# A speech codec's quantiser on one core: the reciprocal of Silu by another ScalarE function, PSUM given out bank by bank, and the order of the work from a table

## The chip, the cores and the metric

The kernel runs on one core of one Trainium2 chip. The core has five engines that run their own instruction queues in order: TensorE (PE in the profile, its weight loads PEld), VectorE (DVE), ScalarE (ACT), GpSimd (POOL) and SyncE (SP); sixteen DMA engines move data between HBM and SBUF. An engine that meets an instruction whose inputs are not there waits, and everything behind it in its queue waits too. The metric is the device time of the one core in microseconds, the median of several runs.

## What is computed

The input is two sequences of 16,000 tokens with 512 channels, in bf16. A depthwise convolution with three taps runs along the tokens, then Silu, then a residual quantiser with four codebooks of eight words, then a second depthwise convolution with three taps over the sum of the chosen words.

```python
z = sum(xp[:, i:i+T, :] * dw_enc[i] for i in range(3))
z = silu(z)
res, q = z, 0
for s in range(4):
    cb = codebooks[s]                      # 8 words of 512 channels
    d2 = |res|^2 - 2 res @ cb.T + |cb|^2
    sel = cb[d2.argmin(-1)]
    q, res = q + sel, res - sel
y = sum(qp[:, i:i+T, :] * dw_dec[i] for i in range(3))
```

## The kernel before

**Tiling.** Each of the 128 partition rows of the token matrix owns 250 consecutive tokens ("groups"). The groups are handled in 17 chunks of SIZES groups (12, thirteen times 16, 12, 12, 6). Within a chunk the 512 channels are four blocks of 128, and in the tiles the channels lie on the partitions.

**Front of a chunk (`load`, `front`).** SyncE issues transposing DMAs from HBM into XT. For each of the four blocks VectorE multiplies XT by the three taps (`product`, L673, into Z and T), and the sums Z + T are made by VectorE (L681) or by an accumulating DMA issued on GpSimd's queue (L679; the table DMA_ADDS says which). Then Silu: ScalarE takes E = Exp(-Z) (L685), VectorE adds one (`one`, L689), ScalarE takes LN = Ln(E) (L693) and E = Exp(-LN) (L696), which is the reciprocal, and VectorE multiplies RES = Z * E (`silu`, L701). The residual RES has three buffers, Z four, T five, E three, LN one. One table set with both Exp and Ln is loaded at the start (L309).

**Four stages of a chunk (`stage`).** In each, TensorE multiplies the residual by itself and by the code words (`score`, L761 and L769, up to six groups per PSUM tile of one bank); VectorE takes the largest entry per token as the norm (`norm`, L789, TR); the products with the words (`dots`, PR) are copied by ScalarE (L795) or by VectorE (L797), as DOTS says: for a chunk of 16 groups the first two pieces of six on ScalarE and the last of four on VectorE. VectorE then adds and takes the minimum (L822, L826, L832) and marks the chosen word (OH, L837). TensorE turns the marks (L848, in the last stage L854), VectorE copies them out of PSUM (`turned`, MT, L861), TensorE expands them (L870; last stage L865), ScalarE cuts them (PH, L879; OHT, L876). In the first three stages the residual is then changed in four blocks: in the blocks below ON_DVE TensorE makes the words (SEL, L906) and VectorE subtracts them (L916); in the others TensorE makes the new residual (NEW, L922 and L927) and ScalarE copies it back in two halves (`keep`, L934, L936). ON_DVE is 3 for all chunks but the last three, where it is 4.

**Output (`finish`, `outputs`).** TensorE multiplies the turned marks by tables of taps times words (Y, L971), ScalarE copies two groups at a time (YSB, L981), and SyncE stores (L984).

**PSUM.** Two pools: psG, two buffers of one bank for the scores, and psA, three buffers of two banks for everything else.

**What sets the order.** Every step is handed to `plan.add` with an engine, a holding time, the steps it needs, a due time and the buffers that it takes and gives. `Plan.run` passes a list scheduler forward and backward over them with the seeds in ROUNDS, shifts the ranks of some steps by the 531 seeds in MOVES, and `emit` then writes the steps out in that order; the engines' queues hold them as emitted. `emit` also fills gaps that the plan sees on TensorE with matmuls whose result is not used (`warm`, L548).

Of the kernel before, what the change touches and what calls it, by code (L numbers as in the profile page):

```python
# [12 lines left out]
F32 = mybir.dt.float32  # L13
# [16 lines left out]
DOTS = (1, 1, 0)  # L30

ON_DVE = [(3, 3, 3)] * 14 + [(4, 4, 4)] * 3
# [11 lines left out]
ZB, TB, EB, LNB, YB = 4, 5, 3, 1, 2  # L44
# [4 lines left out]
ROUNDS = [(11759, 1, 0, 0), (57303, 0.3, 1, 1), (5748, 1, 0.5, 1), (67857, 1, 1, 1), (38131, 0.3, 0, 1),  # L49
          (74597, 0.3, 0, 1)]  # L50

MOVES = [523166, 840848, 180453, 289372, 896190, 468587, 667483, 70738, 572357, 394540, 577496, 170691, 429993,
# [41 lines left out]

CELLS, COLUMNS, ROWS, QUARTERS = range(4)
WHOLE = (CELLS, CELLS, 0, 0.0)
SWITCH, CLING, SLOW = 0.1, 10.0, 1.08
RUNS, ADDS = (1, 1, 0, 0.0), (2, 2, 0, 0.0)
APART, CLUMP = 0.5, 2.0

LAG, SLACK, STORE = 2, 4.5, 0.35


class Plan:

    def __init__(self, slots):
        self.slots = dict(slots)
# [1000 lines left out]
```

## Time and profile before

| | us |
|---|---|
| median of 3 runs | 678.83 |
| lowest, highest | 675.73, 680.55 |
| span of the profiled execution, first to last instruction | 675.1 |
| DVE busy in it | 623.1 |
| ACT busy in it | 599.1 |
| PE busy in it | 541.9 |
| POOL busy in it | 105.4 |

Of the profiled execution only the span is recorded; the median of the runs lies 3.7 us above it, and the lowest run 0.6 us above it.

How to read the profile: a row of a group names the line of the kernel, the engine, the operation, the output and input tiles with their shapes, and the count; behind the first bar stand the microseconds in which the engine was busy with them and the mean of one in nanoseconds, behind the second the idle time of the engine just ahead of them and what ended it. Records on one engine overlap a little, so that the mean of one is larger than the distance from one start to the next.

### The profile page before, as it was taken

The numbers are of one execution on the slowest core, as the hardware profiler recorded it, in microseconds if no ns is written. First come the engines' busy times: TensorE is split into PE (matmuls) and PEld (weight loads), VectorE is DVE, ScalarE is ACT, GpSimd is POOL, SyncE is SP. The second block draws the span as 40 slices with busy tenths as digits, with TensorE's granted clock in tenths as the row PEclk, the third lists the DMA queues.
The fourth block names the chain that finished last, engine by engine and source line by source line (L and its number), as shares of the span: only waits on it lengthen the run. The fifth ranks groups of instructions, "written<-read, shape, count | busy, mean of one in ns | idle before, by whom it ended". The sixth has DMA issues, their size and how long they took to land.

```text
span 675.1 us, 25728 instructions
## 1 busy us (share of the span) xinstructions
PE 541.9 (80%) x11544; PEld 322.8 (48%) x11544; DVE 623.1 (92%) x1256; ACT 599.1 (89%) x615; POOL 105.4 (16%) x147
## 2 busy tenths in 40 slices
PE   6135866888988889797978898979898888989995
PEld 5023534545544535454544455545455455556551
DVE  6999999999999999899989999999999999999861
ACT  4869689999999999999988999999999899777566
POOL 8021112121111111020211102101112211110000
PEclk9668788999999999999999989999999999999998
DMA  6999898999999999999999897989979945353144
GB/s 155 153 199 193 146 195 145 159 230 178 189 235 158 224 201 180 188 241 213 188 198 185 202 187 186 198 185 165 228 140 182 238 78 137 97 126 125 69 182 194
DMA packets 164889, 119.38 MB, mean 177 GB/s; under 512 B 143801, under 2 KB 144186, under 8 KB 164650
## 3 DMA queue, kind: packets, MB, share of 16 engines
q1 hardware_dynamic: 150032, 69.88, 48.3%
q0 software_dynamic: 14464, 47.59, 38.9%
q8 instruction: 90, 1.47, 0.9%
q10 hardware_dynamic: 282, 0.26, 0.1%
q14 instruction: 21, 0.17, 0.1%
HBM read 2.36 MB, written 32.77 MB: 52 GB/s over the span
## 4 chain that ended last, share of the span: by engine, by line
DVE 47%; ACT 19%; DMA 13%; PE 13%; issue 7%; ACTq 0%; DVEq 0%; POOL 0%; POOLq 0%
DVE RES L916 13%; DMA Z<-T 8%; DVE RES L701 7%; DVE T L673 6%; DVE TR L789 6%; PE PS L769 4%; ACT YSB L981 4%; ACT E L696 4%; DVE Z L673 4%; ACT E L685 3%; DVE Z L681 3%; ACT LN L693 3%; DMA XT<-in_x_dram 3%; DVE E L689 3%; ACT RES L934 3%
## 5 line engine op out<-in xcount | busy, mean ns | idle before, releaser
L769 PE MATMUL PS<-RES 128*64 128x80 bf16 (+1 forms) x8064 | 180.3, 203 | 27.7 <-DVE RES L701 9.5
L769 PEld LDWEIGHTS <-RES 128*64 128x64 bf16 x8064 | 174.4, 115 | 38.2 <-DVE RES L916 10.6
L916 DVE TENSOR_TENSOR RES<-RES,SEL 128x2048 bf16<-128x2048 bf16 (+2 forms) x207 | 181.2, 907 | 5.3 <-PE SEL L906 4.8
L679 POOL DMA_DIRECT2D Z<-T x96 | 89.0, 976 | 492.6 <-DVE Z L673 64.2
L981 ACT ACTIVATE YSB<-Y 128x1024 bf16<-128x1024 f32 x126 | 127.1, 1054 | 13.7 <-PE Y L971 12.6
L685 ACT ACTIVATE E<-Z 128x2048 bf16<-128x2048 bf16 (+2 forms) x68 | 123.3, 1814 | 7.9 <-DMA Z<-T 4.2
L693 ACT ACTIVATE LN<-E 128x2048 f32<-128x2048 bf16 (+2 forms) x68 | 123.7, 1820 | 3.5 <-DVE E L689 3.1
L696 ACT ACTIVATE E<-LN 128x2048 bf16<-128x2048 f32 (+2 forms) x68 | 123.1, 1810 | 0.3
L789 DVE TENSOR_REDUCE TR<-PS 128x6 bf16<-128x384 f32 (+1 forms) x188 | 94.4, 506 | 16.3 <-PE PS L769 16.2
L673 DVE TENSOR_SCALAR T<-XT,WENC 128x2048 bf16<-128x2048 bf16 (+2 forms) x136 | 94.7, 706 | 5.8 <-DMA Z<-T 4.2
L934 ACT ACTIVATE RES<-NEW 128x1024 bf16<-128x1024 f32 x78 | 81.6, 1059 | 6.3 <-PE NEW L927 6.1
L701 DVE TENSOR_TENSOR RES<-Z,E 128x2048 bf16<-128x2048 bf16 (+2 forms) x68 | 77.2, 1136 | 0.8 <-ACT E L696 0.7
L906 PE MATMUL SEL<-PH,HIGH 64*128 64x512 bf16 (+2 forms) x324 | 61.6, 374 | 17.0 <-ACT YSB L981 5.9
L761 PE MATMUL PS<-MASK,IDENT 128*64 128x384 bf16 (+1 forms) x376 | 64.3, 337 | 11.8 <-ACT PR L795 6.6
L971 PE MATMUL Y<-S,OHT 64*128 64x512 bf16 (+1 forms) x186 | 55.3, 387 | 9.5 <-DVE RES L916 2.3
L906 PE MATMUL SEL<-PH,LOW 64*128 64x512 bf16 (+2 forms) x324 | 59.7, 360 | 0.0
L906 PE MATMUL SEL<-PH,MID 64*128 64x512 bf16 (+2 forms) x324 | 59.6, 360 | 0.0
L922 PE MATMUL NEW<-RES,IDENT 128*128 128x512 bf16 (+1 forms) x168 | 50.4, 382 | 9.8 <-DVE RES L916 3.4
L971 PE MATMUL Y<-T,OHT 64*128 64x512 bf16 (+1 forms) x187 | 53.7, 386 | 3.7 <-ACT OHT L876 1.8
L761 PEld LDWEIGHTS <-IDENT 128*64 128x64 bf16 x376 | 22.8, 109 | 58.8 <-issue 46.4
L673 DVE TENSOR_SCALAR Z<-XT,WENC 128x2048 bf16<-128x2048 bf16 (+2 forms) x68 | 47.7, 707 | 0.0
L689 DVE TENSOR_SCALAR E<-E 128x2048 bf16<-128x2048 bf16 (+2 forms) x68 | 44.3, 652 | 2.0 <-ACT E L685 1.9
(108 smaller groups left out, 584.2 us busy)
## 6 DMA issues: line engine op xcount, KB each, us to landing
Z<-T POOLq DMA_DIRECT2D x78, 512.0 KB, 6.3
out_dram<-YSB SPq DMA_DIRECT2D x61, 512.0 KB, 4.6
Z<-T POOLq DMA_DIRECT2D x12, 384.0 KB, 6.6
RES<-in_x_dram SPq DMA_DIRECT2D x1, 1664.0 KB, 7.2
Z<-T POOLq DMA_DIRECT2D x6, 256.0 KB, 5.3
XT<-in_x_dram SPq DMA_TRANSPOSE x76, 5.9
out_dram<-YSB SPq DMA_DIRECT2D x1, 384.0 KB, 2.3
out_dram<-YSB SPq DMA_DIRECT2D x1, 256.0 KB, 2.6
```

The lines of the kernel that those rows point to most:

```text
L673: nc.vector.tensor_scalar(out=places(u[name]), in0=taps(i, k), scalar1=WENC[:, i, k:k + 1], scalar2=None, op0=ALU.mult)
L685: nc.scalar.activation(u["E"][:, 0:G, :], u["Z"][:, 0:G, :], ACT.Exp, scale=-1.0)
L693: nc.scalar.activation(u["LN"][:, 0:G, :], u["E"][:, 0:G, :], ACT.Ln)
L696: nc.scalar.activation(u["E"][:, 0:G, :], u["LN"][:, 0:G, :], ACT.Exp, scale=-1.0)
L701: nc.vector.tensor_tensor(out=tokens(st["RES"], i, G), in0=halves(u["Z"]), in1=halves(u["E"]), op=ALU.mult)
L769: nc.tensor.matmul(V[d * HT:(d + 1) * HT, own - left:own + HT + right], lhsT=row[:, at:at + HT], rhs=row[:, at - left:at + HT + right], st ...
L789: nc.vector.tensor_reduce(out=to, in_=both(u["V", q], m, home, HT), axis=AX.X, op=ALU.max)
L906: nc.tensor.matmul(SEL[:, h, 0:W], lhsT=words[side(h), i * P:(i + 1) * P], rhs=u["PH"][side(h), :], start=(k == 0), stop=(k == len(parts) ...
L916: nc.vector.tensor_tensor(out=old, in0=old, in1=new, op=ALU.add)
L934: nc.scalar.activation(old, new.rearrange("p h (n t) -> p (h n) t", t=HT), ACT.Copy)
L971: nc.tensor.matmul(Y[:, h, :], lhsT=lhs()[rows], rhs=DEC[table][rows], start=(a == 0), stop=(a == len(banks[k][h][1]) - 1), skip_group_che ...
L981: nc.scalar.activation(u["YSB"][:, at:at + step * (n - 1) + 1:step, :], u[k][:, 0:n, :], ACT.Copy)
```

## The change

Four things change.

1. Silu's reciprocal: Ln and the second Exp go, and the LN pool with them; one ScalarE instruction with the function Reciprocal, with immediate bias and scale, stands in their place, in place on E. Exp and Reciprocal stand in different table sets, so that the build puts an ACT_TABLE_LOAD at each change from one to the other. The steps now need each other so that the four Exp of a chunk come ahead of its four Reciprocal, and these ahead of the next chunk's Exp: 34 loads in the program, where there was 1. Z has five buffers in place of four, E four in place of three.
2. PSUM is one tile of eight banks. A step says how many banks it holds (`banks`) and which step frees them (`frees`); the table PLACES gives the first bank of each step that takes any. The turned marks and their expansion share one bank, not two.
3. Work moves from VectorE to ScalarE: DOTS becomes (1, 1, 1), so that all pieces of PR are copied by ScalarE (68 more); the copy of the turned marks MT in the last stage goes to ScalarE (TURNED, 17); and in the second stage of five chunks ON_DVE becomes 2, so that five subtractions (L916) become ten copies on ScalarE (L934).
4. The scheduler, ROUNDS and MOVES are gone. A string, RANKS, gives each step a number; the steps are emitted in the order of the numbers. The matmuls of `warm` go into the bank of the step that takes banks next, and there are 41, where there were 65.

```diff
-DOTS = (1, 1, 0)
-ON_DVE = [(3, 3, 3)] * 14 + [(4, 4, 4)] * 3
+DOTS = (1, 1, 1)
+TURNED = (0, 0, 0, 1)
+ON_DVE = [(3, 3, 3), (3, 3, 3), (3, 3, 3), (3, 3, 3), (3, 2, 3), (3, 3, 3), (3, 2, 3), (3, 3, 3), (3, 2, 3), (3, 3, 3), (3, 2, 3), (3, 3, 3), (3, 2, 3), (3, 3, 3), (4, 4, 4), (4, 4, 4), (4, 4, 4)]
-ZB, TB, EB, LNB, YB = 4, 5, 3, 1, 2
+ZB, TB, EB, YB = 5, 5, 4, 2
...
+    def run(self):
+        digit = {c: n for n, c in enumerate(DIGITS)}
+        starts = [UNIT * (len(DIGITS) * digit[a] + digit[b]) for a, b in zip(RANKS[::2], RANKS[1::2])]
+        takers = [n for n, t in enumerate(self.tasks) if t[10]]
+        assert len(starts) == len(self.tasks) and len(takers) == len(PLACES)
+        self.emit(starts, sorted(range(len(starts)), key=lambda n: (starts[n], n)), dict(zip(takers, map(int, PLACES))))
...
-    psG = ctx.enter_context(tc.tile_pool(name="psG", bufs=2, space=bass.MemoryType.PSUM))
-    psA = ctx.enter_context(tc.tile_pool(name="psA", bufs=3, space=bass.MemoryType.PSUM))
-
-    nc.scalar.preload_act_table_set("natural_log_exp_and_others")
+    psum = ctx.enter_context(tc.tile_pool(name="psum", bufs=1, space=bass.MemoryType.PSUM))
+    PS = psum.tile([P, BANKS, 512], F32, name="PS")
+
+    nc.scalar.preload_act_table_set("exp_and_others")
...
-            def log():
-                u["LN"] = lnpool.tile([P, GC, P], F32, name="LN")
-                nc.scalar.activation(u["LN"][:, 0:G, :], u["E"][:, 0:G, :], ACT.Ln)
-
             def inverse():
-                nc.scalar.activation(u["E"][:, 0:G, :], u["LN"][:, 0:G, :], ACT.Exp, scale=-1.0)
+                e = u["E"][:, 0:G, :]
+                zero, unit = (mybir.ImmediateValue(dtype=F32, value=v) for v in (0.0, 1.0))
+                nc.scalar.add_instruction(mybir.InstActivation(
+                    func=ACT.Reciprocal, name=nc.get_next_instruction_name(), engine=mybir.EngineType.Activation,
+                    ins=[nc.scalar.lower_ap(e), zero, unit, zero], outs=[nc.scalar.lower_ap(e)]))
...
-            e = plan.add("ACT", act(1.8), act(1.8) + 0.12, [z], due, exp, take=("E",))
+            e = plan.add("ACT", act(1.8), act(1.8) + 0.12, [z] + kept.get("exps", [])[-1:] + kept.get("inverses", [])[-1:], due, exp,
+                         take=("E",), mode=EXPS)
+            kept.setdefault("exps", []).append(e)
             e = plan.add("DVE", dve(0.6), dve(0.6) + 0.1, [e], due, one)
-            e = plan.add("ACT", act(1.8), act(1.8) + 0.12, [e], due, log, take=("LN",))
-            e = plan.add("ACT", act(1.8), act(1.8) + 0.12, [e], due, inverse, give=("LN",))
...
+            def close():
+                r = plan.add("ACT", act(1.8), act(1.8) + 0.12, [e] + kept["exps"][-1:] + kept.get("inverses", [])[-1:], due, inverse, mode=INVERSES)
+                kept.setdefault("inverses", []).append(r)
...
-        for i in range(KT):
-            block(i)
+        for close in [block(i) for i in range(KT)]:
+            close()
...
-            nc.vector.tensor_copy(u["MT"], u["ps"][:, 0:n])
+            if TURNED[s]:
+                nc.scalar.activation(u["MT"], u["ps"][:, 0:n], ACT.Copy)
+            else:
+                nc.vector.tensor_copy(u["MT"], u["ps"][:, 0:n])
```

ScalarE's queue, from the second Exp of the sixth chunk on. E<-Z is the Exp, LN and E<-LN the Ln and the Exp of before, PR the products with the words, PH the cut marks, YSB the output and RES the copied-back residual. Before:

```order
L685 ACTIVATE E<-Z 128x2048
L934 ACTIVATE RES_94<-NEW 128x16x64
L795 ACTIVATE PR<-PS 128x8x6
L934 ACTIVATE RES_94<-NEW 128x16x64
L696 ACTIVATE E<-LN 128x2048
L879 ACTIVATE PH<-ps_oh 128x512
L693 ACTIVATE LN<-E 128x2048
L685 ACTIVATE E<-Z 128x2048
L795 ACTIVATE PR<-PS 128x8x6
L696 ACTIVATE E<-LN 128x2048
```

In the changed kernel the same place holds these rows; E<-E is the Reciprocal:

```order
L590 ACTIVATE E<-Z 128x2048
L706 ACTIVATE PR<-PS 128x8x6
L896 ACTIVATE YSB<-PS 128x1024
L590 ACTIVATE E<-Z 128x2048
L850 ACTIVATE RES_87<-PS 128x16x64
L706 ACTIVATE PR<-PS 128x8x6 x2
L590 ACTIVATE E<-Z 128x2048
L850 ACTIVATE RES_87<-PS 128x16x64
L706 ACTIVATE PR<-PS 128x8x4
L599 ACT_TABLE_LOAD
L599 ACTIVATE E<-E 128x2048
L706 ACTIVATE PR<-PS 128x8x4
```

Before, the reciprocal of one block stands among the Exp of the next blocks; now the first reciprocal of the chunk stands behind the fourth Exp and a table load, and the small copies PR of four groups stand in this queue.

VectorE's queue from the first product RES<-Z,E of the same chunk past the second. TR, V, KEY, M and OH are the steps from the norm to the marks, and RES<-RES,SEL or RES<-RES,PS the subtraction. Before:

```order
L701 TENSOR_TENSOR RES_94<-Z,E 128x2x16x64
L797 CAST PR<-PS 128x8x4
L673 TENSOR_SCALAR Z<-XT,WENC 128x2048
L822 TENSOR_TENSOR V<-PR,TR 128x128
L701 TENSOR_TENSOR RES_94<-Z,E 128x2x16x64
L916 TENSOR_TENSOR RES_93<-RES_93,SEL 128x2x16x64
L826 TENSOR_TENSOR KEY_132<-V,GWIDE 128x128
L789 TENSOR_REDUCE TR<-PS 128x4
L832 TENSOR_REDUCE M<-KEY_132 128x16
L797 CAST PR<-PS 128x8x4
L789 TENSOR_REDUCE TR<-PS 128x6
```

Now:

```order
L606 TENSOR_TENSOR RES_89<-Z,E 128x2x16x64
L700 TENSOR_REDUCE TR<-PS 128x6
L578 TENSOR_SCALAR Z<-XT,WENC 128x2048
L832 TENSOR_TENSOR RES_88<-RES_88,PS 128x2x16x64
L733 TENSOR_TENSOR V<-PR,TR 128x128
L606 TENSOR_TENSOR RES_89<-Z,E 128x2x16x64
L737 TENSOR_TENSOR KEY_123<-V,GWIDE 128x128
L578 TENSOR_SCALAR Z<-XT,WENC 128x2048
L743 TENSOR_REDUCE M<-KEY_123 128x16
L832 TENSOR_TENSOR RES_88<-RES_88,PS 128x2x16x64
L748 TENSOR_TENSOR OH_124<-KEY_123,M 128x128
L832 TENSOR_TENSOR RES_88<-RES_88,PS 128x2x16x64
```

The copies PR<-PS are gone from VectorE's queue, and V follows the last TR of its stage with work of other chunks between.

More of the change, by code (lines that the diff above doesn't have):

```diff
@@ L110, in __init__, with add @@
         self.part = 0
-    def add(self, engine, hold, delay, needs, due, emit, take=(), give=(), mode=WHOLE):
-        self.tasks.append((engine, hold, delay, [n for n in needs if n is not None], due, emit, take, give, mode, self.part))
+        self.bank = None
+    def add(self, engine, hold, delay, needs, due, emit, take=(), give=(), mode=WHOLE, banks=0, frees=None):
+        self.tasks.append((engine, hold, delay, [n for n in needs if n is not None], due, emit, take, give, mode, self.part, banks, frees))
@@ L245, in emit, with held @@
+    def emit(self, starts, order, place):
+        tasks = self.tasks
+        freed, spans, end = [0.0] * BANKS, [], 0.0
+        takers = [n for n in order if n in place]
+        def held(n):
+            return range(place[n], place[n] + tasks[n][10])
         for n in order:
-            engine, hold, delay, _, _, emit, take, give, _, _ = tasks[n]
+            engine, hold, delay, _, _, emit, _, _, _, _, banks, frees = tasks[n]
             at = starts[n]
@@ L259, in emit @@
                         end += 0.1
-                while back and back[0] <= at:
-                    free += 1
-                    heapq.heappop(back)
                 end = at + hold
                 spans.append((at, end))
-            free -= take.count("psG")
-            for _ in range(give.count("psG")):
-                heapq.heappush(back, at + max(hold, delay))
+            if banks:
+                takers.remove(n)
+                self.bank = place[n]
+                for b in held(n):
+                    freed[b] = 1e9
             emit()
+            if frees is not None:
+                for b in held(n if frees < 0 else frees):
+                    freed[b] = at + max(hold, delay)
 @with_exitstack
@@ L342 @@
     free = {"RES": list(RESB), "KEY": [], "OH": []}
[L343 removed]
+    plan = Plan({"XT": 2, "Z": ZB, "T": TB, "E": EB, "Y": YB, "RES": 3, "KEY": 3,
                  "OH": 3, "PH": PHB})
```

301 lines of the change are left out of this document (116 added, 185 removed), and 40 rows, old and new, of the table MOVES.

## The prediction

> **What bounds the kernel now.** I read the page's busy times and chain first, then a table of busy time by stretch, then what VectorE waits for. The first two lines are the page's; in the table of stretches the columns are the stretch, its length, the busy time of PE, PEld, DVE, ACT and POOL with instruction counts, the granted clock, the DMA engines' busy share and GB/s; the last block is who waited for whom on DVE from 40 to 600 us (total, times, longest).
>
> ```profile
> PE 541.9 (80%) x11544; PEld 322.8 (48%) x11544; DVE 623.1 (92%) x1256; ACT 599.1 (89%) x615; POOL 105.4 (16%) x147
> DVE 47%; ACT 19%; DMA 13%; PE 13%; issue 7%; ACTq 0%; DVEq 0%; POOL 0%; POOLq 0%
> ```
> ```profile
> 0.00:40.00 40.00, 12.74 (x117) 10.18 (x117) 33.18 (x81) 27.92 (x25) 15.56 (x48) 0.77 0.95 165
> 40.00:600.00 560.00, 466.32 (x10118) 275.83 (x10120) 538.47 (x1023) 519.43 (x522) 89.06 (x100) 0.97 0.95 184
> 120.00:520.00 400.00, 342.43 (x7574) 199.31 (x7570) 386.98 (x714) 386.83 (x391) 59.32 (x64) 1.00 1.01 193
> 600.00:675.10 75.10, 62.88 (x1321) 36.77 (x1315) 51.45 (x154) 51.71 (x70) 0.81 (x1) 0.97 0.35 132
> ```
> ```profile
> DVE TR L789 <- PE PS L769: 8.0, 11, 2.3
> DVE T L673 <- DMA Z<-T: 4.2, 3, 2.1
> DVE RES L916 <- PE SEL L906: 3.0, 8, 0.9
> DVE E L689 <- ACT E L685: 1.9, 3, 1.2
> DVE T L673 <- DMA XT<-in_x_dram: 1.5, 1, 1.5
> DVE RES L701 <- ACT E L696: 0.7, 1, 0.7
> DVE V L822 <- ACT PR L795: 0.7, 2, 0.4
> ```
>
> In the settled part, 120 to 520 us, VectorE and ScalarE are both busy for 387 of 400 us: two engines bound the kernel together, and the chain of waits changes between them. VectorE's idle time is 6.8 us before 40 us, 560 - 538.47 = 21.5 us in the middle and 75.1 - 51.45 = 23.7 us at the end, 52.0 us in all, which with 623.1 busy gives the span of 675.1. In the middle no single wait is large: 20.0 of the 21.5 us are the seven rows above, of which ScalarE releases 3.3. The DMA engines' share of 1.01 there says that the transfers are a third resource with little room. TensorE has room: 466 of 560 us.
>
> So a cut on ScalarE alone gives at most the few microseconds in which VectorE waits for it. What sets the gain is what VectorE itself loses.
>
> **VectorE.** The durations; the first rows are groups (busy, mean ns, then the idle time ahead), the others the timeline (start, length), from which the distance between starts is read, since records overlap.
>
> ```profile
> L797 DVE CAST PR<-PS 128x32 bf16<-128x32 f32 x56 | 10.1, 180 | 0.0
> L797 DVE CAST PR<-PS 128x48 bf16<-128x48 f32 x12 | 2.3, 195 | 0.0
> L861 DVE COPY MT<-ps_oh 128x512 bf16<-128x512 bf16 x13 | 5.4, 414 | 0.0
> L916 DVE TENSOR_TENSOR RES<-RES,SEL 128x2048 bf16<-128x2048 bf16 x117 | 140.1, 1212 | 3.4 <-PE SEL L906 3.1
> ```
> ```profile
> 323.23 0.18 DVE L797 CAST PR<-PS 128x32 bf16<-128x32 f32 x1
> 323.33 0.74 DVE L673 TENSOR_SCALAR Z<-XT,WENC 128x2048 bf16<-128x2048 bf16 x1
> ...
> 356.50 1.21 DVE L916 TENSOR_TENSOR RES<-RES,SEL 128x2048 bf16<-128x2048 bf16 x1
> 357.63 0.22 DVE L826 TENSOR_TENSOR KEY<-V,GWIDE 128x128 bf16<-128x128 bf16 x1
> ...
> 365.59 0.41 DVE L861 COPY MT<-ps_oh 128x512 bf16<-128x512 bf16 x1
> 365.92 0.41 DVE L789 TENSOR_REDUCE TR<-PS 128x4 bf16<-128x256 f32 x1
> ```
>
> A PR copy holds VectorE for 323.33 - 323.23 = 0.10 us, though its record is 0.18 long: 56 + 12 = 68 of them give 6.8 us. A copy MT of the last stage holds it for 0.33: 17, four of them smaller, give 5.5. A subtraction holds it for 1.13: five give 5.7. Together 18.0 us; every other VectorE step keeps its count and shape. Its busy time goes from 623.1 to 605.1.
>
> **ScalarE.** The removed Ln, the Exp, the one table load, and the timeline rows for what comes over from VectorE:
>
> ```profile
> L685 ACT ACTIVATE E<-Z 128x2048 bf16<-128x2048 bf16 x52 | 101.2, 1946 | 3.7 <-DMA Z<-T 2.0 <-DVE Z L681 1.6
> L693 ACT ACTIVATE LN<-E 128x2048 f32<-128x2048 bf16 x52 | 101.6, 1954 | 2.9 <-DVE E L689 2.7
> L693 ACT ACTIVATE LN<-E 128x1536 f32<-128x1536 bf16 x12 | 17.9, 1495 | 0.6 <-DVE E L689 0.5
> L693 ACT ACTIVATE LN<-E 128x1024 f32<-128x1024 bf16 x4 | 4.2, 1052 | 0.1
> L309 ACT ACT_TABLE_LOAD x1 | 1.3, 1283 | 0.7 <-PEq L1092 0.7
> ```
> ```profile
> 334.46 0.28 ACT L795 ACTIVATE PR<-PS 128x48 bf16<-128x48 f32 x1
> 334.56 1.99 ACT L693 ACTIVATE LN<-E 128x2048 f32<-128x2048 bf16 x1
> 336.36 0.29 ACT L795 ACTIVATE PR<-PS 128x48 bf16<-128x48 f32 x1
> 336.46 0.68 ACT L879 ACTIVATE PH<-ps_oh 128x512 bf16<-128x512 f32 x1
> 336.93 1.11 ACT L981 ACTIVATE YSB<-Y 128x1024 bf16<-128x1024 f32 x1
> ...
> 339.73 1.13 ACT L934 ACTIVATE RES<-NEW 128x1024 bf16<-128x1024 f32 x1
> 340.63 2.03 ACT L696 ACTIVATE E<-LN 128x2048 bf16<-128x2048 f32 x1
> ```
>
> A full Ln holds ScalarE for 1.80 us, 0.15 less than its mean record; by the same cut the smaller ones hold it for 1.35 and 0.90. So 52 x 1.80 + 12 x 1.35 + 4 x 0.90 = 113.4 us go. The Reciprocal is not in this trace. Ln and Exp, two functions with different output types, take 1954 and 1946 ns for the same tile, so I take it at the price of the second Exp whose place it has, no gain and no loss; the dear end is twice that, as if it ran in two passes, +113.4 us. Thirty-three more table loads cost 33 x 1.283 = 42.3 us if the record is the whole price. The trace has one load, with nothing ahead of it, so what a load costs between two busy instructions it doesn't show; as the dear end I take twice the record, 84.7 us, and below the record nothing, because it was busy that long. I take the record, the only row there is. Added: 68 PR at 0.10 = 6.8 us, 17 MT at no more than a PH's 0.47 = 8.0, ten residual copies at 0.90 = 9.0. The sum is -113.4 + 42.3 + 23.8 = -47.3: from 599.1 to 551.8 us busy, or to 594 at the dear load.
>
> The Trainium skill speaks against the record here: "ScalarE: Activation LUTs", section "What ACT_TABLE_LOAD costs", says that the 1283 ns of a load come with about 1380 ns in which the engine is drained, 2.66 us for each switch. By it 33 loads would cost an estimated 88 us, and ScalarE would stay at about 597. No run here shows the drain so far; the record of 1283 agrees with the first of the two figures.
>
> **Waits.** PR of a stage's last piece now comes from ScalarE. There a PR stands behind whatever is ahead of it in the queue, and on VectorE the step V and all behind it stand behind the PR. Of this wait there were 0.7 us in 2 times with 120 PR on ScalarE; with 188 I take about 1 us, and if ScalarE were late by one Exp (1.80) in each of the 68 stages it could be 122. The new bank plan lets the turned marks hold one bank and not two; what it can win is in the rows where VectorE waits for PS and SEL, 11.0 us together. TensorE gets ten NEW for five SEL and loses 24 unused matmuls; with 94 us of room in the middle I cost that at nothing. No step is added to the DMA queues.
>
> **The sum.** I leave VectorE's idle time at both ends, 6.8 + 23.7 us, since the last chunks keep ON_DVE at 4 and their chain of stages is the same length, and set the middle at 15 us in place of 21.5: the 3.3 that ScalarE released, as it gets 47 us of room, and some 3 of the 11.0 on PE. 605.1 + 6.8 + 23.7 + 15 = 650.6 us of span. The median lies 3.7 us above the span before (678.8 against 675.1), so the time is 654 us.
>
> **The rivals.** The rows for them: the landing time of the adding DMAs (lowest, median, highest), ScalarE's wait for them, and GB/s in 40 slices.
>
> ```profile
> DMA to landing us min/median/max: 3.3/6.2/12.6
> ```
> ```profile
> ACT E L685 <- DMA Z<-T: 4.2, 4, 2.2
> ```
> ```profile
> GB/s 155 153 199 193 146 195 145 159 230 178 189 235 158 224 201 180 188 241 213 188 198 185 202 187 186 198 185 165 228 140 182 238 78 137 97 126 125 69 182 194
> ```
>
> *A better order.* If the new order and the emptier ScalarE take the middle's idle time to 5 us and a third of the 30.5 at the ends, the span is 605.1 + 5 + 20 = 630 to 635: about 637. For it: the waits are small and scattered. Against: 23.7 us of them are at the end, where the last chunk's stages follow each other.
>
> *Dear table loads.* At 2.57 us a load ScalarE stays as full as before (594), nothing in VectorE's middle improves, and some waits grow: 605.1 + 52.0 = 657 to 664 of span, about 663. This is where the Trainium skill's drain would lead too.
>
> *The transfers bind.* The same bytes must move in less time. If the DMA share of 1.01 is the limit, the middle can't shrink, and the time stays near 677. Against it: slices up to 241 GB/s beside a mean of 193, and only 5.7 us of VectorE's waiting is on DMAs.
>
> *Slower: the fourth Exp holds up ScalarE.* All four Exp of a chunk must be issued before its first Reciprocal. The Exp of blocks 2 and 3 wait for two adding DMAs, which land in 6.2 us in the median and 12.6 at worst. When one is late, everything behind it in ScalarE's queue stands: PR, PH and the copied residual that VectorE and TensorE need, and all four Reciprocal, so that four products and with them the Z buffers are late. Before, a late Z held up one block. At 3 us in each of 14 chunks it costs 42 us: 696. It makes the kernel slower from (685.6 - 654) / 14 = 2.3 us a chunk on. For it: the DMA share, and the Z buffers that stay taken through both phases. Against: before, ScalarE waited 4.2 us in all for these DMAs, and there is a fifth Z and a fourth E.
>
> *The exchange doesn't save the Ln.* A Reciprocal at twice an Exp makes ScalarE 551.8 + 113.4 = 665 us busy; with the 12.1 and 23.4 us that it is idle at the ends the time is about 704. Only the missing row speaks for it. The Trainium skill, "ScalarE: Activation LUTs", section "Step-by-step: what each stage is for", has one element a cycle for every function, which by an estimate is the same price as an Exp; the equal rows of Ln and Exp agree.
>
> **The numbers.** A measurement of this kernel can tell 1% from no change: faster is below 672.0, slower above 685.6. Chances: the forecast 0.46 (its own range 645 to 665), the better order 0.17, dear loads 0.10, the transfers 0.11, the held-up queue 0.14, the dear Reciprocal 0.02. Faster are the first three, 0.72 with a hundredth off for the forecast's edge; the transfers' case and that hundredth give 0.12 within 1%; the last two 0.16. The range runs from the lowest end of the better order, 630 + 3.7 = 634, to 678, which takes in the first three cases (0.73) and most of the fourth.
>
> **What would show it.** Right: VectorE busy near 605 and over 97% between 120 and 500 us; ScalarE busy near 552 with 34 loads of 1.28 us and about 0.1 us of idle time around each; Reciprocal records of 1.95 us. Wrong: idle time around the loads of more than 1 us, which is the dear load; ScalarE's Exp waiting for Z<-T over 30 us in all, which is the held-up queue; VectorE's taps waiting for XT or Z<-T with GB/s no higher than 193, which are the transfers; V waiting for PR.

## The result and the profile after

The changed kernel is slower. The median is 682.49 us over 20 runs against 675.39 us over 20 runs of the kernel before on the same chip: a ratio of 1.0143, 95% interval 1.0110 to 1.0177, so 9.7 us more at 675. Ratios are of fast executions alone, those at most 1.5% above the fastest of their kernel (12 of 20 before, 19 of 20 now), and so this one is not the quotient of the two medians, which is 1.0105, or 7.1 us. Slower it is by both. The profiled execution has a span of 679.5 us against 675.1, and so shows 4.4 us of the loss.

The busy times (first line) and the chain that ended last (second line) of the changed kernel:

```profile
PE 537.8 (79%) x11513; PEld 324.4 (48%) x11550; DVE 605.9 (89%) x1166; ACT 555.2 (82%) x675; POOL 102.1 (15%) x147
DVE 40%; ACT 18%; PE 16%; DMA 15%; issue 9%; POOL 1%; SPq 0%; ACTq 0%; DVEq 0%; POOLq 0%
```

Its busy time by stretch, with the columns of the prediction's table:

```profile
0.00:40.00 40.00, 10.80 (x107) 9.91 (x108) 32.23 (x81) 18.62 (x14) 15.58 (x48) 0.69 1.02 165
40.00:600.00 560.00, 457.57 (x9918) 271.96 (x9946) 517.75 (x924) 478.77 (x569) 85.39 (x98) 0.95 0.95 180
120.00:520.00 400.00, 329.23 (x7150) 194.06 (x7176) 362.23 (x629) 349.65 (x414) 53.68 (x60) 0.96 1.00 188
600.00:679.50 79.50, 69.39 (x1490) 42.51 (x1496) 55.91 (x163) 57.85 (x93) 1.16 (x1) 0.96 0.40 151
```

VectorE's busy time is 605.9 us, as the sum had it (605.1), and ScalarE's 555.2 (551.8). What changed is idle time. VectorE's was 6.8, 21.5 and 23.7 us in the three parts of the span; it is now 40 - 32.23 = 7.8, 560 - 517.75 = 42.2 and 79.5 - 55.91 = 23.6. So 17.2 us of work went and 21.6 us of waiting came, nearly all of it (20.7) in the middle: together the 4.4 us between the two spans. Between 120 and 520 us neither engine is full any more: 362 and 350 of 400 us, where both were at 387.

What VectorE waits for in the middle of the changed kernel:

```profile
DVE TR L700 <- PE PS L680: 11.0, 11, 2.1
DVE T L578 <- DMA XT<-in_x_dram: 10.7, 2, 8.6
DVE RES L832 <- PE PS L822: 7.4, 9, 1.6
DVE Z L578 <- DMA XT<-in_x_dram: 5.3, 2, 4.1
DVE V L733 <- ACT PR L706: 1.8, 1, 1.8
DVE RES L606 <- ACT E L599: 1.3, 4, 0.7
DVE Z L586 <- DMA Z<-T: 0.8, 1, 0.8
```

The rows on XT have grown: 10.7 + 5.3 = 16.0 us against 1.5. The longest of them in the timeline of VectorE, with the idle time in brackets, and below it the pieces of the chain of waits that lead there:

```profile
429.42 0.22 DVE L775 COPY MT<-PS 128x128 bf16<-128x128 bf16 x1
438.20 0.75 DVE L578 TENSOR_SCALAR T<-XT,WENC 128x2048 bf16<-128x2048 bf16 x1 [8.56 <-DMA XT<-in_x_dram]
```
```profile
416.71 5.62 DMA Z<-T
422.33 0.02 issue
422.35 15.66 DMA XT<-in_x_dram
```

The transposing load could be issued only when an adding DMA had landed, because the two kinds take turns (`keep_apart`, LAG of 2), and it then took 15.66 us. That is far longer than the median landing of an XT load, 6.4 us. By an estimate from these rows a load of median length would have landed at 422.35 + 6.4 = 428.8, before VectorE was through with its copy at 429.42 + 0.22 = 429.64. So here the slow landing makes the wait, and the turn alone would not have. From 422.35 to 438.01 the DMA engines' busy share was 1.18, and they moved 123 GB/s where the mean from 120 to 520 us is 188. From issue to landing, the longest XT load took 11.1 us before and takes 15.1 here. SyncE's queue shows the waits for the turn over the whole span, a little longer than before; the first row is the changed kernel, the second the kernel before (total, times, longest):

```profile
SPq L507 <- DMA Z<-T: 219.1, 24, 17.9
```
```profile
SPq L602 <- DMA Z<-T: 196.2, 28, 14.8
```

ScalarE's new instructions, by group and then in the timeline around one switch from Exp (E<-Z) to Reciprocal (E<-E):

```profile
L599 ACT ACTIVATE E<-E 128x2048 bf16<-128x2048 bf16 x52 | 99.7, 1924 | 1.0 <-DVE E L594 0.9
L590 ACT ACTIVATE E<-Z 128x2048 bf16<-128x2048 bf16 x52 | 99.5, 1918 | 4.5 <-DVE Z L586 3.0 <-DMA Z<-T 1.3
L599 ACT ACT_TABLE_LOAD x17 | 21.8, 1283 | 0.3
L590 ACT ACT_TABLE_LOAD x16 | 20.5, 1283 | 3.4 <-DVE Z L586 3.0 <-DVE KEY L737 0.2
```
```profile
360.19 0.28 ACT L706 ACTIVATE PR<-PS 128x48 bf16<-128x48 f32 x1
360.49 1.28 ACT L599 ACT_TABLE_LOAD   x1
361.79 1.91 ACT L599 ACTIVATE E<-E 128x2048 bf16<-128x2048 bf16 x1
```

Reciprocal costs what Exp costs, 1924 against 1918 ns, and a load its record: the next instruction starts 361.79 - 360.49 = 1.30 us after it.

### The profile page after: what moved, and what is told of

Its sections match the earlier page's. It is cut to its first block, busy times and chain, and to the rows that moved or that the text cites. A ratio compares the mean times of both kernels' runs of the same rounds, so it can differ in the third digit from the quotient of the medians.

```text
span 679.5 us, 25822 instructions
## 1 busy us (share of the span) xinstructions
PE 537.8 (79%) x11513; PEld 324.4 (48%) x11550; DVE 605.9 (89%) x1166; ACT 555.2 (82%) x675; POOL 102.1 (15%) x147
## 2 busy tenths in 40 slices
DMA packets 164889, 119.38 MB, mean 176 GB/s; under 512 B 143801, under 2 KB 144186, under 8 KB 164650
## 4 chain that ended last, share of the span: by engine, by line
DVE 40%; ACT 18%; PE 16%; DMA 15%; issue 9%; POOL 1%; SPq 0%; ACTq 0%; DVEq 0%; POOLq 0%
DVE RES L832 11%; DMA XT<-in_x_dram 8%; DVE T L578 6%; PE PS L680 6%; DVE TR L700 6%; DMA Z<-T 5%; DVE RES L606 5%; ACT E L599 5%; PE PS L822 4%; ACT E L590 4%; ACT YSB L896 4%; DVE E L594 3%; DVE Z L578 3%; ACT RES L850 2%; DVE Z L586 2%
## 5 line engine op out<-in xcount | busy, mean ns | idle before, releaser
L832 DVE TENSOR_TENSOR RES<-RES,PS 128x2048 bf16<-128x2048 bf16 (+2 forms) x202 | 175.6, 902 | 10.3 <-PE PS L822 9.8
L896 ACT ACTIVATE YSB<-PS 128x1024 bf16<-128x1024 f32 x126 | 124.0, 1031 | 13.6 <-PE PS L886 8.6
L599 ACT ACTIVATE E<-E 128x2048 bf16<-128x2048 bf16 (+2 forms) x68 | 121.7, 1799 | 1.1 <-DVE E L594 0.9
L578 DVE TENSOR_SCALAR T<-XT,WENC 128x2048 bf16<-128x2048 bf16 (+2 forms) x136 | 94.9, 710 | 11.9 <-DMA XT<-in_x_dram 10.7
L850 ACT ACTIVATE RES<-PS 128x1024 bf16<-128x1024 f32 x88 | 89.9, 1032 | 7.4 <-PE PS L843 6.9
L822 PE MATMUL PS<-PH,HIGH 64*128 64x512 bf16 (+2 forms) x314 | 62.2, 381 | 12.2 <-ACT PH L793 4.2
L838 PE MATMUL PS<-RES,IDENT 128*128 128x512 bf16 (+1 forms) x188 | 58.1, 391 | 4.7 <-DVE RES L832 2.0
L822 PE MATMUL PS<-PH,LOW 64*128 64x512 bf16 (+2 forms) x314 | 59.7, 366 | 0.4 <-issue 0.4
L822 PE MATMUL PS<-PH,MID 64*128 64x512 bf16 (+2 forms) x314 | 59.7, 366 | 0.1
L886 PE MATMUL PS<-S,OHT 64*128 64x512 bf16 (+1 forms) x169 | 53.4, 397 | 6.1 <-DVE RES L832 2.7
L886 PE MATMUL PS<-T,OHT 64*128 64x512 bf16 (+1 forms) x170 | 51.9, 395 | 5.5 <-ACT OHT L790 1.8
```

The lines of the kernel that those rows point to most:

```text
L578: nc.vector.tensor_scalar(out=places(u[name]), in0=taps(i, k), scalar1=WENC[:, i, k:k + 1], scalar2=None, op0=ALU.mult)
L599: nc.scalar.add_instruction(mybir.InstActivation(func=ACT.Reciprocal, name=nc.get_next_instruction_name(), engine=mybir.EngineType.Activation,
L822: nc.tensor.matmul(SEL[:, h, 0:W], lhsT=words[side(h), i * P:(i + 1) * P], rhs=u["PH"][side(h), :], start=(k == 0), stop=(k == len(parts) ...
L832: nc.vector.tensor_tensor(out=old, in0=old, in1=new, op=ALU.add)
L850: nc.scalar.activation(old, new.rearrange("p h (n t) -> p (h n) t", t=HT), ACT.Copy)
L886: nc.tensor.matmul(Y[:, h, :], lhsT=lhs()[rows], rhs=DEC[table][rows], start=(a == 0), stop=(a == len(banks[k][h][1]) - 1), skip_group_che ...
```

## The experiments

Eighteen kernels ran, the kernel before beside each. "Ratio" is always to the kernel before; a difference between two runs is the difference of their ratios at 675 us, with the two intervals put together as the root of the sum of squares. The changed kernel stands at 1.0143.

### What of the work matters: loads, VectorE, transfers

**The table loads.** Exp in place of Reciprocal, so that no table is switched; the reciprocal is not computed.

```diff
-                    func=ACT.Reciprocal, name=nc.get_next_instruction_name(), engine=mybir.EngineType.Activation,
+                    func=ACT.Exp, name=nc.get_next_instruction_name(), engine=mybir.EngineType.Activation,
```

> The changed kernel with the function Exp where Reciprocal stood, so that the 33 table switches are gone (42 us of ScalarE) and the order is the same; Silu's reciprocal is not computed. Theory 'switches': 640-665, ratio 0.95-0.985. Theories 'transfers' and 'order': ScalarE's extra room is not used, 676-683, ratio 1.00-1.015.

Ratio 1.0124 (1.0050 to 1.0199): 1.3 us less than the changed kernel, plus or minus 5.6, with ScalarE at 516.3 us in place of 555.2. VectorE's waits for XT stay at 15.4 us. The switches as such are not what costs.

**VectorE and ScalarE lighter, in both kernels.** The subtractions and the copies of the residual work on half of the tokens (the other half keeps the residual of the stage before).

```diff
+                old = old[:, :, :, 0:HT // 2]
...
-                nc.scalar.activation(old, new.rearrange("p h (n t) -> p (h n) t", t=HT), ACT.Copy)
+                nc.scalar.activation(old[:, :, 0:HT // 2], new.rearrange("p h (n t) -> p (h n) t", t=HT)[:, :, 0:HT // 2], ACT.Copy)
```

> The changed kernel with the subtraction on VectorE and the residual copy on ScalarE over the first half of the tokens only, in the same order and with all DMAs: about 75 us less on VectorE and 38 less on ScalarE; the other half of the residual isn't changed. Theory 'transfers': the middle is held by the DMAs and hardly shrinks, 660-680, ratio 0.98-1.01. Theory 'order' or an engine as the bound: VectorE's cut shows for the most part, 610-645, ratio 0.90-0.955.

> The kernel before with the same halves left out. Theory 'transfers': it falls to the same floor as the changed kernel, 650-672, ratio 0.965-0.995, so that 75 us less on VectorE bring less than 25. Without a floor by the DMAs: 610-640, ratio 0.90-0.95.

The changed kernel: ratio 0.9950 (0.9910 to 0.9990). The kernel before: 0.9635 (0.9556 to 0.9714). Their busy lines, the changed kernel's first:

```profile
PE 538.7 (80%) x11513; PEld 320.9 (48%) x11550; DVE 540.2 (81%) x1166; ACT 520.9 (78%) x675; POOL 102.2 (15%) x147
```
```profile
PE 529.6 (82%) x11495; PEld 322.6 (50%) x11544; DVE 554.0 (86%) x1256; ACT 565.9 (88%) x615; POOL 106.6 (17%) x147
```

Both land where the theory of the transfers had them, the second just below its range. Two things follow. In the kernel before, 623.1 - 554.0 = 69.1 us less on VectorE (and 33 less on ScalarE) bring 24.6 us (plus or minus 5.3): VectorE alone does not bound it, and a microsecond taken from it is worth about 0.36, in an order of steps that was made for the full work (a new order for the light kernel was not tried). In the changed kernel 65.7 us less bring 13.0 (plus or minus 3.6), 0.20 for one, and with less work on both engines than the light kernel before it is 21 us slower. Both move the same bytes: the kernel before does so in a span of 645.1 us, so the transfers' capacity is no floor at 670. Something in the changed kernel holds it there that is neither an engine's work nor the sum of the bytes.

**The adding DMAs halved, in both kernels.** Only the first half of each tile is added.

```diff
-                    keep_apart(nc.gpsimd.dma_start(out=z, in_=t, accum_op=ALU.add), adds, runs)
+                    keep_apart(nc.gpsimd.dma_start(out=z[:, 0:G // 2, :], in_=t[:, 0:G // 2, :], accum_op=ALU.add), adds, runs)
```

> The changed kernel with the adding DMAs over the first half of each tile only: the same number of DMAs, half of their bytes (about 24 of 119 MB less); the other half of these sums is left out. Theory 'transfers': VectorE's 17 us come out and more, 645-665, ratio 0.955-0.985. Theory 'order': 674-682, ratio 1.00-1.012. 'Switches': as 'order'.

> The kernel before, with the adding DMAs over the first half of each tile only, the control to the same edit of the changed kernel. Theory 'transfers': before was bound by VectorE and ScalarE, so little goes: 665-673, ratio 0.985-0.998, and the changed kernel with the same edit is faster than this one. Theory 'order': about the same fall as in the changed kernel, which stays 5-10 us above this one.

Ratios 0.9672 (0.9589 to 0.9754) and 0.9878 (0.9796 to 0.9960): 31.8 us from the changed kernel, 8.2 from the kernel before, as the theory of the transfers had it. The changed kernel's middle with half the adding DMAs:

```profile
40.00:600.00 560.00, 477.27 (x10630) 285.24 (x10632) 542.50 (x994) 500.37 (x609) 89.62 (x99) 0.98 0.72 144
```

VectorE now idles 17.5 us there and not 42.2, and the changed kernel is 13.9 us (plus or minus 7.9) under the kernel before with the same halving. That is near the 17.2 us of work that VectorE lost: a gain is there as soon as the adding DMAs leave room.

**Which adding DMAs.** Blocks 0 and 1 of a chunk have one each, blocks 2 and 3 two. Halved for block 3 alone, or for blocks 0 and 1 alone: in both a third of the adding bytes loses its half. The first run's edit; the second has `i < 2`:

```diff
-                    keep_apart(nc.gpsimd.dma_start(out=z, in_=t, accum_op=ALU.add), adds, runs)
+                    m = G // 2 if i == 3 else G
+                    keep_apart(nc.gpsimd.dma_start(out=z[:, 0:m, :], in_=t[:, 0:m, :], accum_op=ALU.add), adds, runs)
```

> The changed kernel; the two adding transfers of the fourth token block of every chunk add the first half of the tile only (the other half of the transposed positions is not added). A third of the adding bytes goes. 'Z loop' (the next chunk's Z products wait for this chunk's Silu, whose four reciprocals wait for the fourth Exp, and that for two adding transfers one after the other): the loop gets shorter by two half transfers a chunk, so 12 to 25 us of the 29 us that halving all of them saved: 655 to 668 us. 'Bytes' (the transfers' capacity): a third of the 29 us, about 670 us, the same as the next run. 'VectorE binds': under 3 us.

> The changed kernel; the single adding transfers of the first two token blocks of every chunk (in the kernel's program these two blocks have fewer adding transfers than the last two) add the first half of the tile only. The same number of bytes goes as in the run before if each has one. 'Z loop': these Z are early and the fourth Exp does not wait for them: 0 to 5 us, 674 to 681 us. 'Bytes': as in the run before, about 670 us.

Ratios 0.9912 (0.9864 to 0.9960) and 0.9900 (0.9824 to 0.9976), 15.6 and 16.4 us less than the changed kernel. The theory of the Z loop had the second at 0 to 5 us and is wrong there: it makes no difference whose DMAs are shorter. That the two are alike is what the theory of the bytes had; by it each would be a third of the 31.8 us that halving all of them brought, 10.6, and both are somewhat more. VectorE's waits in the middle with blocks 0 and 1 halved:

```profile
DVE TR L701 <- PE PS L681: 12.5, 10, 2.7
DVE RES L833 <- PE PS L823: 7.7, 9, 1.6
DVE V L734 <- ACT PR L707: 2.4, 2, 1.9
DVE E L595 <- ACT E L591: 2.1, 4, 1.3
DVE T L578 <- issue: 1.1, 1, 1.1
DVE RES L607 <- ACT E L600: 1.0, 2, 0.7
DVE T L578 <- DMA Z<-T: 0.4, 1, 0.4
```

The waits for XT (16.0 us) are gone in both runs, those for TensorE are about as they were (18.4 us, here 20.2), and the time falls by the same 16 us. The longest landing of an XT load is 11.1 and 10.1 us, as in the kernel before or less. So the late XT loads are a place where this kernel loses, and it did not matter which third of the adding bytes was halved. The kernel before was not run with these two edits; with all adding DMAs halved it gained 8.2 us, so some of the 16 us it might gain too.

**The turns.** A transpose waits until the fourth-last adding DMA has landed, in place of the second-last, and the other way round.

```diff
-LAG, SLACK, STORE = 2, 4.5, 0.35
+LAG, SLACK, STORE = 4, 4.5, 0.35
```

> The changed kernel, with the take-turns rule between transposing and adding DMAs loosened: each waits for the fourth one back of the other kind, not the second (LAG 4 for 2). Theory 'transfers' (XT comes late because transposes stand behind adds that stand behind VectorE): VectorE's wait for XT falls from 16 us to under 5 and the time from 682 to 665-673, ratio to before 0.985-0.997. Theory 'order' (the fixed order loses the time in hand-overs between TensorE, ScalarE and VectorE): 679-685, ratio 1.007-1.018. Theory 'switches' (table loads and the four-and-four order on ScalarE): the same, 679-685.

Ratio 1.0764 (1.0662 to 1.0866), 41.9 us slower than the changed kernel; no theory had that. VectorE's waits for XT are gone, as the theory of the transfers had it, and SyncE waits less for its turn (95.0 us in place of 219.1), but the transfers get slower. Their issues, with count, size and the median time to landing, first in this run, then in the changed kernel:

```profile
Z<-T POOLq DMA_DIRECT2D x78, 512.0 KB, 7.6
...
XT<-in_x_dram SPq DMA_TRANSPOSE x76, 9.7
```
```profile
Z<-T POOLq DMA_DIRECT2D x78, 512.0 KB, 6.7
...
XT<-in_x_dram SPq DMA_TRANSPOSE x76, 6.4
```

ScalarE's Exp now waits 35.6 us for Z<-T (first row), where it was 1.5 in the changed kernel (second row), and VectorE's taps wait 20.9 us for it in the middle (third row, of this run):

```profile
ACT E L590 <- DMA Z<-T: 35.6, 8, 8.5
```
```profile
ACT E L590 <- DMA Z<-T: 1.5, 2, 1.3
```
```profile
DVE T L578 <- DMA Z<-T: 20.9, 7, 8.2
```

The turns cost waiting, but less than they save.

**Work back to VectorE.** PR of the last piece and MT back on VectorE; in another run one adding DMA in six back on VectorE.

```diff
-DOTS = (1, 1, 1)
-TURNED = (0, 0, 0, 1)
+DOTS = (1, 1, 0)
+TURNED = (0, 0, 0, 0)
```
```diff
-DMA_ADDS = [((), ())] + [((0, 1, 2, 3), (2, 3))] * 16
+DMA_ADDS = [((), ())] + [((0, 1, 2, 3), (3,))] * 16
```

> The changed kernel with one part undone in the same order of steps: PR of the last piece and MT of the last stage are copied by VectorE again (12 us more on VectorE, 15 less on ScalarE). Theory 'transfers': VectorE's time isn't what is short, 680-686, ratio 1.005-1.02, unchanged within 4 us. Theory 'VectorE binds' (the one of the prediction): 690-697, ratio 1.022-1.034.

> The changed kernel with the last sum Z + T of the third block taken from the DMAs and given to VectorE in 16 chunks (DMA_ADDS (3,) for (2, 3)): 16 adding DMAs less, about 17 us more on VectorE. Theory 'transfers': with a third of what halving all adds took off the DMAs, 669-677, ratio 0.992-1.004, below the changed kernel. Theory 'VectorE binds': 692-700, ratio 1.026-1.038.

Ratios 1.0270 (1.0164 to 1.0376) and 1.0251 (1.0165 to 1.0337). The first gives VectorE 12.3 us more and is 8.6 us slower (plus or minus 7.5): what was moved to ScalarE did not do the harm. The value lies in the range of 'VectorE binds' and over that of the transfers, though its uncertainty reaches both: work given back to VectorE costs 0.70 us for one, though work taken from it gained only 0.20. The second takes the XT waits away but gives VectorE 15.7 us more, and is 7.3 us slower (plus or minus 6.2): VectorE has too little room to take the additions over. That too is near 'VectorE binds' and over the range of the transfers, so neither theory holds for all of these runs: the late loads cost, and VectorE's work still counts.

### Batches, Z buffers and order under the old plan

To part the batches of four from the table and the single PSUM banks, the kernel before got parts 1 and 3 of the change only, with its own scheduler and pools and a new search of ROUNDS and MOVES.

**Batched, and not.** The second kernel has Exp in place of Reciprocal (not computed), so that no load and no batch is needed. Its Exp need no longer follow one another, and the first Silu product of a chunk is kept behind that of the chunk before.

```diff
-        for close in [block(i) for i in range(KT)]:
-            close()
+        for i in range(KT):
+            block(i)()
```

> The kernel before with its own planner, its PSUM pools and a new search of its order, and with two parts of the change: ScalarE's Reciprocal with four Exp and then four Reciprocal in a chunk, one more buffer for Z and for E, and the shifted copies (dot products, turned indices, subtraction). 'Z loop': the batching costs under this planner too: 670 to 690 us although VectorE has 18 us and ScalarE 47 us less to do than in the kernel before. 'Order and banks' (the new table and the single PSUM banks make the changed kernel slow): with the old plan the saving shows, 645 to 662 us.

> As the run before, with the same planner and an own search of the same length, but Exp stands in for Reciprocal (so no table changes and no batches: each block's second pass follows its own first; the reciprocal is not computed). Against the run before this takes away the batches and 42 us of table loads on ScalarE. 'Z loop': 640 to 660 us and at least 15 us under the run before. 'Order and banks': within 8 us of the run before (the loads alone had saved nothing in the changed kernel).

Ratios 1.0446 (1.0374 to 1.0519) and 0.9867 (0.9781 to 0.9953): 39.1 us apart, plus or minus 7.6, each some way above the range of the theory of the Z loop. So the batched Silu is dear without the new table and the single banks too; the table even does better than this search, 1.0143 against 1.0446. The second kernel also shows what the moved work is worth without the batches and loads: 15.4 us less on VectorE and 83.6 less on ScalarE than in the kernel before bring 9.0 us (plus or minus 5.8).

**A second order, and no loads.** Another seed of the same search; and e11's own order with Exp for Reciprocal (not computed).

> The kernel of e11_old_plan_batched with another order from the same search (another seed), nothing else: how far two orders of the same search lie apart. If differences of 10 us and more between the runs under the old plan mean something: 698 to 712 us. If the order found decides: further off than that, to either side.

> The batched kernel under the old plan (e11_old_plan_batched), instruction for instruction, with Exp in place of Reciprocal, so that no tables are switched (the reciprocal is not computed); the batches and their order stay. e11 and e12 differed by 39 us; this run parts the loads from the batches. 'Batches' (Z loop): 695 to 707 us, as e11, as the loads alone saved nothing in the changed kernel. 'Loads' (42 us of ScalarE, placed where the chain is tight): 664 to 680 us.

Ratios 1.0400 (1.0307 to 1.0494), 3 us from the first order, and 1.0340 (1.0255 to 1.0425), 7.2 us (plus or minus 7.5). The four executions of the second lie between 697.4 and 715.0 us. By this the loads account for some 7 of the 39 us, and that is no clear difference.

**Z given back after its Exp.** Silu's product reads E twice (the Silu is not computed).

```diff
-                nc.vector.tensor_tensor(out=tokens(st["RES"], i, G), in0=halves(u["Z"]), in1=halves(u["E"]), op=ALU.mult)
+                nc.vector.tensor_tensor(out=tokens(st["RES"], i, G), in0=halves(u["E"]), in1=halves(u["E"]), op=ALU.mult)
```

> The batched kernel under the old plan, where Silu's product reads E twice (E times E in place of Z times E, the Silu is not computed), so that a Z buffer is free as soon as its Exp has read it and not after Silu; tables, batches, counts and sizes of all instructions stay; own search of the order. 'Z loop' (the next chunk's Z products wait for this chunk's Silu through the five Z buffers): 660 to 685 us, 20 us or more under e11. 'Batches, but not through Z' (the wait for the fourth Exp itself, or orders that are tight elsewhere): 695 to 710 us.

Ratio 1.0049 (1.0006 to 1.0092): 26.8 us under e11, plus or minus 5.7, as the theory of the Z loop had it. VectorE's waits for DMAs in the middle of e11:

```profile
DVE T L633 <- DMA Z<-T: 10.2, 9, 2.7
DVE T L633 <- DMA XT<-in_x_dram: 5.8, 2, 5.2
DVE Z L641 <- DMA Z<-T: 4.1, 2, 2.5
```

Of these 20.1 us only 4.1, for Z<-T, are left in the profile of this run, though it is of the longest of its executions, 690.5 us. So under the old plan much of the cost of the batches goes with the early return of Z, and with it most of the waits for adding DMAs and those for XT. One control is missing. This run frees Z earlier than the kernel before does too, and no run gave Z back early without batches, so a part of the 26.8 us may be a gain that any kernel would have.

**Pairs.** Two Exp, two Reciprocal: 66 loads and not 33.

```diff
-        for close in [block(i) for i in range(KT)]:
-            close()
+        for i in range(0, KT, 2):
+            for close in [block(i), block(i + 1)]:
+                close()
```

> The batched kernel under the old plan with two Exp and then two Reciprocal in place of four and four: 66 table loads in place of 33, so ScalarE has 42 us more to do (about 598 us), VectorE the same; own search of the order. 'Batches' (a block's second pass waits for the fourth block's adding transfers, and its Z buffer is held so long): at least 10 us under e11, 680 to 695 us, in spite of the loads. 'Loads': 10 to 42 us over e11, 715 us or more.

Ratio 1.0370 (1.0302 to 1.0438), 5.1 us under e11 (plus or minus 6.7) although ScalarE is busy for 599.5 us and not 556.9. Less than the 10 us that the theory of the batches asked for, and far from the 10 to 42 us that dear loads would have added. Inconclusive on the size.

### The same in the changed kernel

**Another order; another order with Z given back.** RANKS was replaced by an order searched for long landing times of the DMAs; the second run also has the product E times E (the Silu is not computed).

> The changed kernel with another table of starting times, nothing else: the same instructions, tables, batches, buffers and PSUM banks, in an order found by an own search that lets no transfer land early (the longest landings are counted in). 'The table' (its order sets off the waits, and the batches as such cost nothing): 655 to 670 us. 'Z loop' (batches of four on five Z buffers cost in any order): 672 to 690 us, as the changed kernel.

> As the run before, with Silu's product reading E twice (E times E in place of Z times E, the Silu is not computed), so that a Z buffer is free after its Exp and not after Silu, and with an own search of the same kind and length; instructions and sizes are the same. 'Z loop': 10 us or more under the run before, as under the old plan (e15 against e11, 27 us). 'The table': within 5 us of the run before.

Ratios 1.0094 (1.0055 to 1.0133) and 1.0029 (0.9993 to 1.0066). The new order gains 3.3 us, plus or minus 3.5. VectorE's waits in the middle show what became of the late loads:

```profile
DVE RES L832 <- PE PS L822: 14.0, 11, 3.5
DVE TR L700 <- PE PS L680: 8.4, 6, 4.9
DVE MT L775 <- PE PS L759: 2.4, 3, 2.0
DVE TR L700 <- ACT E L590: 2.0, 1, 2.0
DVE T L578 <- DMA XT<-in_x_dram: 1.6, 1, 1.6
DVE Z L586 <- DMA Z<-T: 1.1, 1, 1.1
DVE E L594 <- ACT E L590: 0.7, 2, 0.5
```

The wait for XT is 1.6 us and no longer 16.0, but the wait for the subtractions' words has grown from 7.4 to 14.0, and the time hardly moved: an order can push the wait to another place, which the shorter transfers did not do. Giving Z back takes another 4.4 us (plus or minus 3.6), less than the 10 us that the theory of the Z loop asked for and within the 5 us of 'the table'; but that theory had the new order itself at 655 to 670 us, and it stays at 682. Neither theory holds in full. None of the kernels that compute everything beat the kernel before.

## Why the prediction was wrong

**VectorE's and ScalarE's own work: right.** 605.9 against 605.1 us and 555.2 against 551.8. The idle time at both ends was right too, 7.8 and 23.6 us against 6.8 and 23.7. A load costs its record of 1.283 us, and the Reciprocal an Exp. The rivals of dear loads and of a dear Reciprocal fall with these rows, and e2 shows that even all the loads together are worth 1.3 us (plus or minus 5.6). The Trainium skill, "ScalarE: Activation LUTs", section "What ACT_TABLE_LOAD costs", adds a drain of about 1380 ns to each switch; this trace does not show it, with 0.3 us of idle time ahead of 17 loads, 3.4 ahead of the other 16, 3.0 of these by VectorE, and the next instruction 1.30 us after the start of one.

**The step that failed: "What sets the gain is what VectorE itself loses", and from it the sum that sets the middle's idle time at 15 us in place of 21.5.** It was 42.2. VectorE's idle time was taken as fixed beside its work. Run e6 shows that it isn't, even in the kernel before: with 69.1 us less work the time falls by 24.6 and the rest turns into waiting. At 0.36, by an estimate, the 17.2 us that VectorE lost were worth some 6 us and not 18, still on the right side; e12, without loads and batches, has 9.0 us for 15.4. VectorE was busy for 362 of 400 us between 120 and 520, 91%, and not over 97. The profile before had hinted at it, with ScalarE at the same 387 of 400 us and the DMA engines' share at 1.01; ScalarE was given its due in the sum, the transfers were not. The 3.7 us from span to median came from three executions; over 20 the median before lies 0.3 us above its profiled span and the changed kernel's 3.0, so that term did not decide it.

**The price of the batches was set at nothing.** The step above makes the gain smaller; a loss needs something more. The sum costed the loads and the Reciprocal, but not that four Z stay taken until the fourth Exp and a load are through. Measured 9.7 us slower where some 6 us faster were to be had, the change cost about 16 us more than its work says (13 by the medians). That the batches are the cause is shown under the old plan, and only in part here. The held Z buffers were named in the rival of the held-up queue, one of the two that had the kernel slower, but tied to the wrong wait: ScalarE's Exp waits 1.5 us for Z<-T, not over 30. What is late is the XT loads, and with them VectorE's taps, 16.0 us. SyncE's turn behind the adding DMAs has grown less, from 196.2 to 219.1 us over the span, and the longest of the waits comes from a load that took 15.66 us.

**The rival of the transfers has its sign, with the wrong reason and size.** It gave 677 us, no change, and the sign "VectorE's taps waiting for XT or Z<-T with GB/s no higher than 193"; there were 16.2 us of such waits at 188 GB/s. It was set aside because of slices up to 241 GB/s and because only 5.7 us of VectorE's waiting was on DMAs before. The sum of the bytes, of which it spoke, is not the limit: e6 moves the same 119.38 MB in a span of 645.1 us. What is left is when adding DMAs and transposes meet: the stretch of 15.66 us above has full DMA engines and a load that lands late, e1 slows both kinds by letting more of them overlap, and e9 and e10 win 16 us by shortening either third. That is an argument from these runs together; none moves the same bytes at other times and nothing else.

**What is shown, and what stays open.** Shown: the loss lies in waiting and not in work; the table loads are a small part; the 16.0 us of waits for XT go when one third of the adding DMAs is halved, whichever of the two; under the old plan the batched Silu with its loads costs 39 us, and 27 of these go when Z is given back early. Not settled is why the XT loads are late in the changed kernel. There giving Z back brings 4.4 us, another order 3.3 and the absence of loads 1.3, each with an uncertainty of about its size or more; added up, which assumes that they are independent, that is some 9 of the 16 us. The rest may be the wait of each Reciprocal for the fourth Exp itself, or the new PSUM plan; no run took away either in the changed kernel. A kernel with more Z buffers that computes everything was not tried.

## What to carry to other kernels

Where two engines and the DMA queues are all near nine tenths busy, a microsecond saved on the fullest need not be a microsecond: lighten that engine alone and see what comes of it before a plan is built on its sum. When a change groups work to save table switches, price how long the group holds its buffers and follow that one step further, to the loads that share the DMA engines with the additions which those buffers feed. A wait that vanishes from its row in a new order has not been won until the total has moved.

## What the hardware showed unexpectedly

Letting transposing loads and adding DMAs overlap more (e1, LAG 4 in place of 2) slowed both: XT from 6.4 to 9.7 us to landing, Z<-T from 6.7 to 7.6, and the kernel by 42 us, with the same packets and bytes. The Trainium skill, "DMA: Bandwidth & Descriptors", section "Rules for kernel authors", says that a transpose next to ordinary DMAs needs nothing. It says so beside transposes that corrupt each other, and gives no time; for the time, this run says otherwise.

TensorE's granted clock between 120 and 520 us is 0.96 where it was 1.00, with 329 us of work where there were 342, and 0.92 with 316 us in e1. The two do not go together strictly: e10 has 343 us at 0.97. Whether part of a wait is paid twice through the clock, no run here parts from the rest.
